# One core, cross attention and max-out FFN: batch 0's tokens by the hardware queue, batch 2's through the array, and one token load per period

## Chip, cores, metric

One core of one Trainium2 chip. The metric is the device time of one execution in microseconds (us). Each kernel was run several times; runs are sorted into a fast and a slow state, and only fast runs are compared. The profile's span is mostly 1.7 to 2.1 us shorter than the time of the same run (168.5 against 170.3 for the kernel before, 158.2 against 160.2 for an experiment), so spans are compared with spans and times with times.

## The reference

```python
# x (8, 8, 512, 64), state (8, 8, 32, 64): batch, head, rows, depth
scores  = softmax(x @ state^T / 8)        ; xread = scores @ state     # 512 rows a batch
scores2 = softmax(state @ x^T / 8)        ; sread = scores2 @ x        # 32 rows a batch
rows = concat(xread, sread), heads side by side  -> (4352, 512)
h = max(rows @ w1, rows @ w2, rows @ w3)  # 512 -> 768
out = h @ w_out                           # 768 -> 512, fp32
```

## The kernel before

The program is a list of small units that are issued in a fixed order; every engine works through its own part of that order. For batch b: `lx` loads the tokens (fp32 in HBM, bf16 in SBUF, a casting DMA issued by POOL); `pm` permutes them in SBUF; then they are transposed, by a DMA on SP's queue (`xb`) or by PE and an eviction (`xT`); `S` makes half the scores, their exponentials `e`, sums and probabilities `a`; `ab` (in a period `X`) transposes the probabilities by a DMA, `aT` by PE; `M b m` folds state and weights into M; `u` is one of three up-projections of a block of 128 hidden columns; `o` half of an output tile; `R` reads the tokens for the state rows.

```python
PERIOD = """
o o u u u u S S o o M M m u R u o u o X u u u u u u u P u u o u o u m M M
"""
...
    def load_x(b):                                    # casting DMA, issued by POOL
        nc.gpsimd.dma_start(
            out=x_sb[:, b].rearrange("p h j d -> p h (j d)"),
            in_=x[b].rearrange("h (p j) d -> p h (j d)", j=J))
...
    def x_crossbar(b):                                # xb: tokens, SP's queue
        nc.sync.dma_start_transpose(
            out=xT(b).rearrange("p j hp t -> p (j hp) t"),
            in_=x_nat(b).rearrange("p j h d -> p (j h d)"))
...
    def a_crossbar(b):                                # ab / X: probabilities, SP's queue
        nc.sync.dma_start_transpose(
            out=aT(b).rearrange("p j a t -> p (j a) t"),
            in_=a_of(b).rearrange("p j a hp n -> p (j a hp n)"))
...
    for t in range(1, B):
        p, g = ORDER[t], ORDER[t + 1]                 # outputs of p, up-projections of g
        nb = t + 2                                    # scores and transposes of nb
        ...
            elif what == "P":
                if nb + 1 < B:
                    permute_x(nb + 1, None, "g")      # a copy on POOL
                    x_crossbar(nb + 1)
            elif what == "X":
                a_crossbar(nb)
```

All eight token loads stand in the opening, before the first period; batch 2's tokens are transposed by a DMA.

The softmax here doesn't subtract the row's maximum and nothing guards it: scores larger than these inputs give would overflow.

Of the kernel before, what the change touches and what calls it, by code (L numbers as in the profile page):

```python
# [8 lines left out]
F32 = mybir.dt.float32  # L9
BF16 = mybir.dt.bfloat16  # L10
# [15 lines left out]


OPENING = """
id, idle 9, sel, idle 9, lx 0, lw 0 1, lx 1, pm 0 0 v, lw 4 6, pm 0 1 g, lw 1 2,
xT 0 0 v, xT 0 1 v, pm 1 0 g, pm 1 1 g, S 0 0 v, M 2 0 aa, S 0 1 v, M 1 0 aa, idle 4,  # L30
lw 2 4, lx 2, M 0 0 aa, aT 0 0 v, R 0, xT 1 0 a, lx 3, aT 0 1 a, xT 1 1 v, S 1 0 g,
u 0 0 0, M 0 4 aa, M 0 5 av, u 0 0 1, u 0 0 2, S 1 1 g, lo, u 0 4 0, u 0 5 0, M 0 1 aa,
u 0 5 1, u 0 4 1, u 0 5 2, M 1 1 aa, u 0 4 2, M 1 4 aa, u 0 1 0, pm 2 - g, aT 1 - v,
xb 2, u 0 1 1, M 0 3 va, M 0 2 va, u 0 1 2, u 1 0 0, u 1 4 0, lx 7, pm 3 - g, u 1 1 0,
lx 6, u 1 0 1, u 0 3 0, u 1 4 1, u 0 2 0, M 1 2 aa, M 1 5 av, xb 3, u 1 4 2, u 0 2 1,
u 1 0 2, u 0 2 2, M 1 3 aa, M 2 3 aa, u 0 3 1, u 0 3 2, u 1 1 1, u 1 2 0, u 1 3 0,
u 1 5 0, u 1 1 2, u 1 5 1, lx 4, u 1 5 2, o 0 0 0 a, o 0 0 1 a, u 1 2 1, S 2 1 g,
S 2 0 g, ab 2, u 1 3 1, o 0 1 0 v, M 2 2 aa, R 1, o 0 1 1 a, o 0 2 0 v, M 2 4 aa,
u 1 2 2, o 0 2 1 a, o 0 3 0 a, M 2 5 aa, M 2 1 va, u 1 3 2, o 0 3 1 v, R 2, lx 5
"""  # L40


PERIOD = """
o o u u u u S S o o M M m u R u o u o X u u u u u u u P u u o u o u m M M
"""
LAST = """
M M u u u M u u S M u u u u u S u u u u P M R M u o u o u u o X o o o o o
"""


# [1 line left out]
def kernel(  # L52
# [14 lines left out]
    nc = tc.nc  # L67

    B, H, S, D = x.shape
# [5 lines left out]
    J = S // 128  # L75
# [6 lines left out]

    const = ctx.enter_context(tc.tile_pool(name="const", bufs=1))
    res = ctx.enter_context(tc.tile_pool(name="res", bufs=1))
    xnp = ctx.enter_context(tc.tile_pool(name="xnp", bufs=3))
    att2 = ctx.enter_context(tc.tile_pool(name="att2", bufs=2))
    tmpp = ctx.enter_context(tc.tile_pool(name="tmpp", bufs=4))
    htp = ctx.enter_context(tc.tile_pool(name="htp", bufs=2))
    op = ctx.enter_context(tc.tile_pool(name="op", bufs=2))
# [3 lines left out]
    def bank(shape, dt, name):  # L93
        return psum.tile(shape, dt, tag="bank", name=name)
# [3 lines left out]
    def copy(eng, o, i):  # L98
        if eng == "a":
            nc.scalar.copy(out=o, in_=i)  # L100
        else:
            ENG[eng].tensor_copy(out=o, in_=i)  # L102

    def mm(out_ap, lhsT, rhs, start, stop, pos=(0, 0)):
        nc.tensor.matmul(out_ap, lhsT, rhs, start=start, stop=stop, tile_position=pos)  # L105

    def tr(out_ap, in_ap):
# [8 lines left out]
    nc.sync.dma_start(  # L116
        out=st32.rearrange("p n d -> p (n d)"),
        in_=state.rearrange("b h (q n) d -> (b h q) (n d)", q=2))
    zeros = const.tile([128, 512], BF16, name="zeros")
    nc.vector.memset(zeros, 0.0)  # L120
    sbd = res.tile([128, B, HP, 2, Ns], BF16, name="sbd")
# [7 lines left out]

    W = res.tile([128, 3, HP, d_ff], BF16, name="W")  # L130
    wout = res.tile([128, MT, d_model], BF16, name="wout")
    x_sb = res.tile([128, B, H, J, D], BF16, name="x_sb")
    M_sb = res.tile([128, B, MT, 2, 3, 128], BF16, name="M_sb")
    AT = res.tile([128, HP, ST], BF16, name="AT")
    w_v = [w.rearrange("(kk p) f -> p kk f", p=128) for w in (moe_w1, moe_w2, moe_w3)]
# [6 lines left out]
    def load_wout():  # L142
        nc.gpsimd.dma_start(out=wout, in_=moe_w_out.rearrange("(kk p) f -> p kk f", p=128))

    def load_x(b):
        nc.gpsimd.dma_start(  # L146
            out=x_sb[:, b].rearrange("p h j d -> p h (j d)"),
            in_=x[b].rearrange("h (p j) d -> p h (j d)", j=J))


# [36 lines left out]
    def tile_of(kind, b, pool, shape):  # L187
        if (kind, b) not in tiles:
            tiles[kind, b] = pool.tile(shape, BF16, tag=kind, name=kind)
        return tiles[kind, b]  # L190

    def x_nat(b):
        return tile_of("xn", b, xnp, [128, J, H, D])

    def xT(b):
        return tile_of("xT", b, att2, [128, J, HP, 128])
# [9 lines left out]

    def permute_x(b, h, eng):
        j = slice(0, J) if h is None else slice(2 * h, 2 * h + 2)
        copy(eng, x_nat(b)[:, j], x_sb[:, b, :, j].rearrange("p h j d -> p j h d"))

    def x_crossbar(b):
        nc.sync.dma_start_transpose(
            out=xT(b).rearrange("p j hp t -> p (j hp) t"),
            in_=x_nat(b).rearrange("p j h d -> p (j h d)"))
# [27 lines left out]
    def a_crossbar(b):  # L242
# [3 lines that stand above are left out]
# [32 lines left out]
    def up(g, m, i):  # L278

        nn = S if g < B else ST  # L280
        ht = tile_of("ht", g, htp, [128, MT, S])
        pw = bank([128, S], F32, "pw")
        if g < B:
            for par in range(2):
                mm(pw, M_sb[:, g, m, par, i, :], aT(g)[:, :, par, :], par == 0, par == 1)
        else:
            for hp in range(HP):
                mm(pw[:, :nn], W[:, i, hp, m * 128:(m + 1) * 128], AT[:, hp, :],
                   hp == 0, hp == HP - 1)
        if i == 0:  # L290
            t = tiles["t", g, m] = tmpp.tile([128, S], BF16, tag="t0", name="t0")
            nc.scalar.copy(out=t[:, :nn], in_=pw[:, :nn])  # L292
        elif i == 1:
            t0 = tiles["t", g, m]
            t = tiles["t", g, m] = tmpp.tile([128, S], BF16, tag="t1", name="t1")
            nc.vector.tensor_max(t[:, :nn], t0[:, :nn], pw[:, :nn])  # L296
        else:
            nc.vector.tensor_max(ht[:, m, :nn], tiles["t", g, m][:, :nn], pw[:, :nn])  # L298

    def out_half(g, j, h, eng):  # L300
        last = g == ORDER[-1]
        if h == 0:
            tiles["po"] = bank([128, d_model], F32, "po")
        po = tiles["po"]
        for kt in range(3 * h, 3 * h + 3):
            mm(po, tiles["ht", g][:, kt, j * 128:(j + 1) * 128], wout[:, kt, :],
               kt == 0, kt == MT - 1)
        if h == 0:
            return
        rows = out[g * SP:g * SP + S, :].rearrange("(p j) f -> j p f", j=J) if g < B else None  # L310
        if last and j == J - 1:
            half = d_model // 2
            for k in range(2):
                o = op.tile([128, half], F32, tag=f"oh{k}", name=f"oh{k}")
                f = slice(k * half, k * half + half)
                copy("av"[k], o, po[:, f])
                (nc.scalar, nc.sync)[k].dma_start(out=rows[j][:, f], in_=o)
            return
        if j % 2 == 0:
            tiles["o"] = op.tile([128, 2, d_model], F32, tag="o", name="o")  # L320
        o = tiles["o"]
        copy(eng, o[:, j % 2, :], po)
        if last:
            nc.sync.dma_start(out=rows[j], in_=o[:, j % 2, :])
        elif g < B:
            if j % 2 == 1:
                nc.sync.dma_start(out=rows[j - 1:j + 1].rearrange("j p f -> p j f"), in_=o)
        else:
            for q in range(4):
                bb = 4 * j + q  # L330
                nc.sync.dma_start(out=out[bb * SP + S:(bb + 1) * SP, :],
                                  in_=o[q * 32:(q + 1) * 32, j % 2, :])
# [46 lines left out]
    for t in range(1, B):  # L379
        p, g = ORDER[t], ORDER[t + 1]  # L380
        nb = t + 2
        us = [(g, m, i) for m in range(MT) for i in range(3)]
        os = [(p, j, h) for j in range(J if p < B else ST // 128) for h in range(2)]
        sc = [0, 1]
        for what in (PERIOD if g != ORDER[-1] else LAST).split():
            if what == "u":
                up(*us.pop(0))
            elif what == "o":
                if os:
                    out_half(*os.pop(0), "a")  # L390
            elif what in ("M", "m"):
                if m_q:
                    m_unit(*m_q.pop(0), "aa" if what == "M" else "av")
            elif nb >= B:
                continue
            elif what == "S":
                scores(nb, sc.pop(0), "g")
            elif what == "P":
                if nb + 1 < B:
                    permute_x(nb + 1, None, "g")  # L400
                    x_crossbar(nb + 1)
            elif what == "R":
                state_reads(nb)
            elif what == "X":
                a_crossbar(nb)
    for j in range(J):
        for h in range(2):
            out_half(ORDER[-1], j, h, "a")
# [29 lines left out]
```

## Time and profile before

| | before |
|---|---|
| time, median (range) | 168.4 us (168.0 to 170.9) |
| span of the profile | 168.5 us (of a run of 170.3 us) |
| PE's longest wait | 7.5 us, for the tokens' DMA transpose `xT` in the opening |
| a steady period | 15.77 us, PE busy 15.66 |
| DMA transposes, median from issue to landing | `xT` 3.8 us, `aT` 3.2 us |

The lines are in the prediction below. A period is bound by PE, the opening by a full DMA and the one transpose that arrives late in it.

### The profile page before, as it was taken

The page shows a single profiled execution, that of the slowest core. Times are in us where ns is not written, and L with a number is a line of the kernel's source. Part 1 is how long each engine was busy: PE and PEld are TensorE (multiplying, and loading weights), DVE is VectorE, ACT ScalarE, POOL GpSimd, SP SyncE. Part 2 cuts the span into 40 slices and gives each one's busy share as a digit, 9 for nine tenths or more (in the row PEclk, how much of TensorE's full clock was granted, in tenths as well). Part 3 has the DMA queues.
Part 4 walks back from the last instruction along what each step waited for, and adds up shares of the span by engine and source line. Part 5 has one row for each costly group of instructions (what it writes and reads, how often), then busy time and mean ns, then how long its engine had stood idle before and what let it go on. Part 6 is the DMA issues. An engine that isn't in the chain of part 4 may idle for free.

```text
span 168.5 us, 3476 instructions
## 1 busy us (share of the span) xinstructions
PE 151.6 (90%) x1353; PEld 74.9 (44%) x1370; DVE 109.0 (65%) x194; ACT 92.9 (55%) x190; POOL 46.7 (28%) x50
## 2 busy tenths in 40 slices
PE   7958999990299989999999999999999999999991
PEld 2435443430243545445445544454455456854440
DVE  2349998971055759949984987498579843559601
ACT  3427987750135286488548755874785473344340
POOL 8876962920060009003500620080013000000000
PEclk9999999998559999999999999999999999999997
DMA  4999999999999904631633382249306033030163
GB/s 133 152 175 196 179 178 197 191 126 126 149 188 146 289 21 160 152 128 69 163 83 124 128 157 67 87 151 168 126 4 187 0 124 127 1 124 0 45 198 132
DMA packets 37536, 21.71 MB, mean 129 GB/s; under 512 B 22672, under 2 KB 34960, under 8 KB 37520
## 3 DMA queue, kind: packets, MB, share of 16 engines
q0 software_dynamic: 15440, 7.34, 35.5%
q1 hardware_dynamic: 21936, 14.03, 33.4%
q8 instruction: 10, 0.16, 0.5%
q10 hardware_dynamic: 144, 0.13, 0.2%
q14 instruction: 6, 0.05, 0.2%
HBM read 15.20 MB, written 8.91 MB: 143 GB/s over the span
## 4 chain that ended last, share of the span: by engine, by line
PE 76%; DMA 16%; POOL 4%; issue 1%; DVE 1%; ACT 1%; POOLq 0%; DVEq 0%; ACTq 0%
PE pw L105 39%; PE po L105 25%; DMA xT<-xn 9%; DMA W<-in_moe_w_dram 7%; PE pm L105 6%; PE pr L105 4%; POOL W L140 2%; PE ps L105 2%; POOL x_sb L146 1%; DVE ht L298 0%; DVE t L296 0%; ACT t L292 0%; PE pa L108 0%; DVE oh L102 0%; ACT oh L100 0%
## 5 line engine op out<-in xcount | busy, mean ns | idle before, releaser
L105 PE MATMUL pw<-aT,M_sb 128*128 128x512 bf16 x288 | 71.3, 381 | 0.1
L105 PE MATMUL po<-wout,ht 128*128 128x512 bf16 x189 | 50.9, 384 | 1.0 <-issue 0.3
L296 DVE TENSOR_TENSOR t<-t,pw 128x512 bf16<-128x512 bf16 (+1 forms) x54 | 35.1, 652 | 22.4 <-ACT t L292 14.0
L292 ACT CAST t<-pw 128x512 bf16<-128x512 f32 (+1 forms) x54 | 30.1, 570 | 27.8 <-PE pw L105 27.5
L105 PEld LDWEIGHTS <-M_sb 128*128 128x128 bf16 x288 | 26.5, 98 | 32.5 <-issue 3.7
L298 DVE TENSOR_TENSOR ht<-t,pw 128x512 bf16<-128x512 bf16 (+1 forms) x54 | 35.3, 657 | 7.1 <-PE pw L105 3.4
L100 ACT CAST M_sb<-pm 128x384 bf16<-128x384 f32 x81 | 33.2, 504 | 5.3 <-PE pm L105 5.3
L238 POOL TENSOR_TENSOR a<-e,rden 128x512 bf16<-128x512 bf16 x14 | 14.4, 1044 | 73.0 <-ACT e L230 46.8
L100 ACT COPY o<-po 128x512 f32<-128x512 f32 x32 | 19.1, 596 | 21.1 <-PE po L105 16.4
L105 PEld LDWEIGHTS <-ht 128*128 128x128 bf16 x204 | 19.3, 99 | 22.7 <-issue 2.9
L102 POOL COPY xn<-x_sb 128x2048 bf16<-128x2048 bf16 (+1 forms) x9 | 15.1, 1687 | 7.4 <-DMA x_sb<-in_x_dram 7.2
L230 ACT ACTIVATE e<-ps 128x512 bf16<-128x512 f32 x16 | 9.0, 605 | 13.0 <-PE ps L105 12.9
L234 DVE TENSOR_REDUCE den<-e 128x16 f32<-128x512 bf16 x16 | 10.6, 663 | 8.5 <-ACT e L230 8.3
L105 PE MATMUL pm<-W,sbd 64*32 64x384 bf16 x384 | 12.7, 331 | 0.6 <-DVE ht L298 0.4
L105 PE MATMUL ps<-sbd,xT 128*128 128x64 bf16 x128 | 5.8, 199 | 7.6 <-DMA xT<-xn 7.5
L105 PEld LDWEIGHTS <-xT 128*128 128x128 bf16 x128 | 5.2, 102 | 9.8 <-DMA xT<-xn 8.0
L105 PEld LDWEIGHTS <-sbd 64*32 64x32 bf16 x384 | 4.3, 90 | 10.9 <-issue 10.2
L140 POOL DMA_DIRECT2D W<-in_moe_w_dram x12 | 9.0, 766 | 0.0
L105 PE MATMUL pw<-AT,W 128*128 128x256 bf16 x72 | 8.8, 273 | 0.0
L102 DVE CAST M_sb<-pm 128x384 bf16<-128x384 f32 x15 | 7.8, 529 | 1.3 <-PE pm L105 1.3
L271 DVE RECIPROCAL rd<-pr 128x128 f32<-128x128 f32 x8 | 7.6, 950 | 1.6 <-PE pr L105 1.4
L105 PE MATMUL pz<-zeros 128*128 128x512 bf16 x20 | 6.9, 495 | 1.2 <-DVE zeros L120 1.2
(38 smaller groups left out, 66.3 us busy)
## 6 DMA issues: line engine op xcount, KB each, us to landing
out_dram<-o SPq DMA_DIRECT2D x14, 512.0 KB, 2.6
x_sb<-in_x_dram POOLq DMA_DIRECT2D x8, 512.0 KB, 10.4
W<-in_moe_w_dram POOLq DMA_DIRECT2D x6, 256.0 KB, 8.2
W<-in_moe_w_dram POOLq DMA_DIRECT2D x6, 128.0 KB, 8.0
wout<-in_moe_w_out_dram POOLq DMA_DIRECT2D x1, 768.0 KB, 12.0
out_dram<-o SPq DMA_DIRECT2D x3, 256.0 KB, 2.1
st<-in_state_dram SPq DMA_DIRECT2D x1, 512.0 KB, 3.4
out_dram<-o SPq DMA_DIRECT2D x8, 64.0 KB, 1.7
```

The lines of the kernel that those rows point to most:

```text
L100: nc.scalar.copy(out=o, in_=i)
L102: ENG[eng].tensor_copy(out=o, in_=i)
L105: nc.tensor.matmul(out_ap, lhsT, rhs, start=start, stop=stop, tile_position=pos)
L140: nc.gpsimd.dma_start(out=W[:, i, :, c], in_=w_v[i][:, :, c])
L146: nc.gpsimd.dma_start(out=x_sb[:, b].rearrange("p h j d -> p h (j d)"), in_=x[b].rearrange("h (p j) d -> p h (j d)", j=J))
L230: nc.scalar.activation(out=e.rearrange("p r n -> p (r n)"), in_=ps.rearrange("p j a hp n -> p (j a hp n)"), func=AF.Exp, scale=scale)
L234: nc.vector.reduce_sum(out=den, in_=e, axis=AX.X)
L238: ENG[eng].tensor_mul(out=a_of(b)[:, 2 * h:2 * h + 2].rearrange("p j a hp n -> p (j a hp) n"), in0=e, in1=rden.unsqueeze(2).to_broadcast(( ...
L271: nc.vector.reciprocal(out=rd, in_=pd.rearrange("p (hp n) -> p hp n", hp=HP))
L292: nc.scalar.copy(out=t[:, :nn], in_=pw[:, :nn])
L296: nc.vector.tensor_max(t[:, :nn], t0[:, :nn], pw[:, :nn])
L298: nc.vector.tensor_max(ht[:, m, :nn], tiles["t", g, m][:, :nn], pw[:, :nn])
```

## The change

Its intent: take the late transpose away (batch 2 through the array), start earlier (batch 0 by the free hardware queue), and free the DMA in the opening (batches 4 to 7 are loaded one per period). Cut to its core (the opening's order, not shown in full, moves many units, and the last period's order changes too; four token buffers in place of eight):

```diff
 OPENING
-id, idle 9, sel, idle 9, lx 0, lw 0 1, lx 1, ... xb 2, ... lx 7, ... lx 6, ... lx 4, ... lx 5
+id, idle 9, sel, idle 9, pm 0 1 v, pm 0 0 a, ... lx 1, ... lx 2, ... lx 3, ... xT 2 1 v, ... xT 2 0 a, ...
 PERIOD
-o o u u u u S S o o M M m u R u o u o X u u u u u u u P u u o u o u m M M
+L u S u o S P u u o u o u u u u u o u o o u u m M m u X R o u u o u m m m u
+    xlp = ctx.enter_context(tc.tile_pool(name="xlp", bufs=4))
+    x32 = res.tile([128, H, J, D], F32, name="x32")
+    nc.sync.dma_start(out=x32.rearrange("p h j d -> p h (j d)"),
+                      in_=x[0].rearrange("h (p j) d -> p h (j d)", j=J))
     def load_x(b):
+        x_sb[b] = xlp.tile([128, H, J, D], BF16, tag="x", name="x")
         nc.gpsimd.dma_start(
-            out=x_sb[:, b].rearrange("p h j d -> p h (j d)"),
+            out=x_sb[b].rearrange("p h j d -> p h (j d)"),
     def permute_x(b, h, eng):
-        copy(eng, x_nat(b)[:, j], x_sb[:, b, :, j].rearrange("p h j d -> p j h d"))
+        i = x_sb[b][:, :, j] if b else x32[:, :, j]
+        copy(eng, x_nat(b)[:, j], i.rearrange("p h j d -> p j h d"))
+            elif what == "L":
+                if nb + 1 < B:
+                    load_x(nb + 1)
```

Note two things in the new period: `L` comes first in the text, and `P` (permute and transpose of the next batch's tokens) now comes ahead of `X` (transpose of the probabilities).

More of the change, by code (lines that the diff above doesn't have):

```diff
@@ L28 @@
 OPENING = """
-id, idle 9, sel, idle 9, lx 0, lw 0 1, lx 1, pm 0 0 v, lw 4 6, pm 0 1 g, lw 1 2,
-xT 0 0 v, xT 0 1 v, pm 1 0 g, pm 1 1 g, S 0 0 v, M 2 0 aa, S 0 1 v, M 1 0 aa, idle 4,
-lw 2 4, lx 2, M 0 0 aa, aT 0 0 v, R 0, xT 1 0 a, lx 3, aT 0 1 a, xT 1 1 v, S 1 0 g,
-u 0 0 0, M 0 4 aa, M 0 5 av, u 0 0 1, u 0 0 2, S 1 1 g, lo, u 0 4 0, u 0 5 0, M 0 1 aa,
-u 0 5 1, u 0 4 1, u 0 5 2, M 1 1 aa, u 0 4 2, M 1 4 aa, u 0 1 0, pm 2 - g, aT 1 - v,
-xb 2, u 0 1 1, M 0 3 va, M 0 2 va, u 0 1 2, u 1 0 0, u 1 4 0, lx 7, pm 3 - g, u 1 1 0,
-lx 6, u 1 0 1, u 0 3 0, u 1 4 1, u 0 2 0, M 1 2 aa, M 1 5 av, xb 3, u 1 4 2, u 0 2 1,
-u 1 0 2, u 0 2 2, M 1 3 aa, M 2 3 aa, u 0 3 1, u 0 3 2, u 1 1 1, u 1 2 0, u 1 3 0,
-u 1 5 0, u 1 1 2, u 1 5 1, lx 4, u 1 5 2, o 0 0 0 a, o 0 0 1 a, u 1 2 1, S 2 1 g,
-S 2 0 g, ab 2, u 1 3 1, o 0 1 0 v, M 2 2 aa, R 1, o 0 1 1 a, o 0 2 0 v, M 2 4 aa,
-u 1 2 2, o 0 2 1 a, o 0 3 0 a, M 2 5 aa, M 2 1 va, u 1 3 2, o 0 3 1 v, R 2, lx 5
+id, idle 9, sel, idle 9, pm 0 1 v, pm 0 0 a, xT 0 0 v, xT 0 1 v, lx 1, idle 3, pm 1 1 v,
+lw 4 6, lw 0 1, pm 1 0 v, lw 2 4, S 0 0 g, lx 2, S 0 1 g, xT 1 1 a, R 0, xT 1 0 a,
+S 1 1 g, S 1 0 g, lw 1 2, lo, M 1 5 aa, M 0 5 aa, aT 0 0 v, aT 0 1 v, M 0 4 aa, M 1 0 av,
+M 0 0 vv, u 0 5 0, aT 1 - v, u 0 4 0, M 2 4 av, M 1 4 aa, u 0 5 1, lx 3, u 0 0 0,
+u 0 4 1, u 0 5 2, u 1 0 0, M 0 2 va, M 0 3 aa, u 0 0 1, u 0 0 2, pm 2 - g, u 1 0 1,
+u 0 2 0, M 1 3 aa, u 0 4 2, u 0 2 1, u 1 4 0, u 0 3 0, u 0 3 1, M 0 1 aa, u 1 4 1,
+xT 2 1 v, u 1 3 0, M 2 5 va, M 1 2 aa, pm 3 - g, u 1 0 2, u 1 4 2, u 0 1 0, xT 2 0 a,
+u 1 5 0, u 0 3 2, u 0 2 2, u 0 1 1, u 1 2 0, u 0 1 2, S 2 0 g, xb 3, M 2 0 aa, M 1 1 aa,
+u 1 3 1, u 1 2 1, o 0 0 0 v, S 2 1 g, o 0 0 1 v, u 1 5 1, M 2 2 aa, u 1 1 0, u 1 5 2,
+o 0 1 0 v, ab 2, o 0 1 1 a, R 1, u 1 3 2, u 1 1 1, o 0 2 0 a, u 1 1 2, u 1 2 2,
+o 0 2 1 a, M 2 1 av, M 2 3 aa, R 2, o 0 3 0 a, o 0 3 1 a
 """
 PERIOD = """
-o o u u u u S S o o M M m u R u o u o X u u u u u u u P u u o u o u m M M
+L u S u o S P u u o u o u u u u u o u o o u u m M m u X R o u u o u m m m u
 """
 LAST = """
-M M u u u M u u S M u u u u u S u u u u P M R M u o u o u u o X o o o o o
+X u u u u u u u M u u L u P u u u o o u M M M R u S u u S M o u o o M o o o
 """
@@ L131 @@
     wout = res.tile([128, MT, d_model], BF16, name="wout")
-    x_sb = res.tile([128, B, H, J, D], BF16, name="x_sb")
     M_sb = res.tile([128, B, MT, 2, 3, 128], BF16, name="M_sb")
@@ L143, in load_wout @@
         nc.gpsimd.dma_start(out=wout, in_=moe_w_out.rearrange("(kk p) f -> p kk f", p=128))
+    x_sb = {}
     def load_x(b):
+        x_sb[b] = xlp.tile([128, H, J, D], BF16, tag="x", name="x")
         nc.gpsimd.dma_start(
-            out=x_sb[:, b].rearrange("p h j d -> p h (j d)"),
+            out=x_sb[b].rearrange("p h j d -> p h (j d)"),
             in_=x[b].rearrange("h (p j) d -> p h (j d)", j=J))
@@ L313, in out_half @@
             for k in range(2):
-                o = op.tile([128, half], F32, tag=f"oh{k}", name=f"oh{k}")
+                o = res.tile([128, half], F32, name=f"oh{k}")
                 f = slice(k * half, k * half + half)
```

## The prediction

> **What bounds the kernel now.** I read the page's slices first, then the chain of work that ended last, then who waited for whom, then the stages in windows, then the DMA views.
>
> ```profile
> PE   7958999990299989999999999999999999999991
> PEclk9999999998559999999999999999999999999997
> DMA  4999999999999904631633382249306033030163
> ```
>
> Each slice is 4.2 us. PE is full except at the start and in slices 10 and 11 (38 to 46 us), after which its clock falls to half. The DMA engines are full from 4 to about 58 us, and mostly free afterwards. So there is one hole, at the end of a stage in which the DMA is saturated. The chain and the waits of PE say what the hole is:
>
> ```profile
> 29.69 0.55 PE pw L105 x3
> 30.24 14.89 DMA xT<-xn
> 45.17 1.03 PE ps L105 x16
> ...
> PE ps L105 <- DMA xT<-xn: 7.5, 1, 7.5
> ```
>
> The scores of batch 2 wait 7.5 us for their transposed tokens, which a DMA transpose, issued at 30.2 us, delivers only 15 us later. The queue table and the issues say why (columns: size, median us from issue to landing):
>
> ```profile
> q0 software_dynamic: 15440, 7.34, 35.5%
> q1 hardware_dynamic: 21936, 14.03, 33.4%
> ...
> x_sb<-in_x_dram POOLq DMA_DIRECT2D x8, 512.0 KB, 10.4
> ...
> xT<-xn SPq DMA_TRANSPOSE x6, 3.8
> ```
>
> A transpose usually lands in 3.8 us; this one shared the engines with the casting loads of batches 7 and 6, queued at 30 to 35 us, which nobody needs for another 40 us or more. The stages (columns: length, then busy time of PE, PEld, DVE, ACT, POOL, then clock, DMA and GB/s):
>
> ```profile
> 9.94:37.68 27.74, 26.48 (x290) 12.56 (x292) 24.10 (x42) 20.02 (x43) 18.67 (x19) 1.00 1.45 178
> 37.68:45.17 7.49, 0.01 (x2) 0.01 (x1) 0.69 (x1) 0.20 (x1) 0.00 (x0) 0.69 1.50 132
> 45.17:56.46 11.29, 10.96 (x120) 5.62 (x121) 6.35 (x12) 5.22 (x11) 2.93 (x3) 0.75 1.29 177
> 56.46:72.94 16.48, 15.94 (x151) 7.54 (x149) 12.65 (x23) 8.66 (x18) 3.87 (x3) 1.00 0.47 137
> 72.94:88.71 15.77, 15.66 (x155) 7.43 (x149) 12.05 (x22) 10.58 (x23) 3.88 (x3) 1.00 0.41 117
> ```
>
> These are the opening before the hole, the hole, the rest of the opening, the first period and a steady one. A period is PE-bound: 15.66 of 15.77 us.
>
> **PE's work at full clock**, from the start-to-start times of full runs in the chain: a up-projection pair of matmuls ("u") 0.431 us (18 matmuls in 3.88), an output half ("o") 0.647, a unit of M 0.203 (24 pm in 0.61), a half of scores 0.235, the state reads of a batch 0.81, an array transpose of half a batch 0.45, of the probabilities 0.41 a batch, a filler matmul 0.216. A period is 18 u, 8 o, 6 M, 2 S and 1 R: 7.76 + 5.18 + 1.22 + 0.47 + 0.81 = 15.4 us, against 15.77 measured; 0.3 us are gaps. The opening from its first array transpose (9.94 us) on holds 36 u, 8 o, 18 M, 6 S, 3 R, 4 array halves, two batches of probabilities and 4 fillers: 31.7 us. It took 46.5 us (9.94 to 56.46). Of the 14.8 us lost, 7.5 are the hole; the half clock after it made 8.1 us of work last 11.3, so 3.2; some 4.1 are lost before the hole, where DVE is 87% busy and the weights are still arriving.
>
> **What the Trainium skill says.** "TensorE: Matmul & The Clock Gate", Part 1, says that the array drops to half clock after an idle window of about 3.4 us and needs about as long a busy one to recover. The trace agrees: after 7.5 us without a matmul the granted clock is 0.55 in 40 to 45 us and 0.50 in 45 to 50 us. "DMA: Bandwidth & Descriptors", Issuing engines are not separate DMA queues, says that DMAs of all engines run on the same 16 DMA engines and interleave; the trace agrees (15 us against 3.8 us for the same transpose). The same page, SWDGE vs HWDGE vs iDMA, says that only a GpSimd DMA can cast, so tokens that come by the hardware queue must be cast on the core; all casting loads of the trace are on POOL's queue. "VectorE: DVE Perf Modes", The perf-mode tier table, gives 1227 ns for an fp32 copy of 2048 elements in SBUF; for the half batch of 1024 I estimate from it 0.7 us. The trace has no such copy, but ACT's fp32 cast of 128x1024 took 1.04 us.
>
> **The change, part by part.**
>
> *Batch 2 through the array.* It removes the DMA transpose that PE waited for. It adds two array halves, 0.9 us of PE and 0.69 us of DVE plus 1.0 us of ACT for the evictions. Removed: 7.5 us of hole and, as no idle of over 3.4 us should remain, the 3.2 us of half clock. Net about -9.8 us.
>
> *Loads of batches 4 to 7 one per period.* The software queue moved four token loads (1024 packets each), all the weights and w_out by 50 us. From the landings I read (batch 0 at 9.5 us, the third weight group at 18.4, batch 2 at 28.3) it serves 1000 packets in about 2.4 us after a start near 6.6 us. The new opening asks 9984 packets of it, so it is done at some 30 to 32 us. Batch 2 lands at 22 to 25 us; PE reaches its transposes at about 26 to 28. Batch 3 lands at 30 to 32, its permute takes 1.9 us on POOL, and its transpose, now in free engines, 3.8: it lands by 38, and PE asks for it at about 45. In the periods a load has no producer to wait for, so POOL issues it right after the previous permute, some 8 to 10 us before its own permute; with free engines I expect it to land in 6 to 8 us. Nothing on the path, but close.
>
> *Batch 0 by the hardware queue.* The state's 0.5 MB was issued at 0.74 us and landed 3.4 us later; 1 MB behind it should land at 7 to 8 us (twice the bytes at about the state's rate, beside the first software load). The casts take 0.7 us (DVE) and 1.05 us (ACT), side by side. So the first array transpose starts near 8.6 us instead of 9.94: 1.3 us sooner. But what follows needs weights: the first M units need 2560 packets (13 to 15 us), the third kind 4096 (16 to 18.5). DVE has some 10 us of work of its own before the first u, too. I put the first u at about 17.5 us, where it was 17.6, but with 5.4 us of PE work done before it, 0.2 us more than before.
>
> *The order.* After the first u the new opening has 32.35 - 5.6 = 26.8 us of PE work and about 24 us of DVE (36 us listed in all by unit durations, 10 before the first u, times 0.945 because instructions overlap in the trace). With some 1 to 1.5 us of gaps it ends at 45 to 46 us. Before, it ended at 56.5. That is -10.5 to -11.5: the 9.8 of the first part, and about 1 from a better order. In the periods three more M copies go from ACT to DVE: 3 x 0.53 brings DVE to 13.6 of 15.8 us, ACT down to 9.1. PE remains the bound; I leave the period at 15.8 us. Before, five periods took 79.5 us (the first one 0.7 longer), and from 136.0 to the end 32.5. Sum: 45.7 + 79.5 + 32.5 = 157.7; with 0.2 from the profile to the median (168.5 to 168.7) and a little for the risks below, 158.3 us.
>
> **Rivals.** *The hole only moves.* The weights wanted late (units of M 1) land at 26 to 28 us, and PE reaches them at about the same time; or 1 MB of fp32 delays all of the software queue by up to 2.4 us (1024 packets' time), and PE stands at the first M units. For it: the DMA engines stay full until 30 us. Against it: PE's order puts each weight group as late as it can. It would cost 2 to 4 us, and a gap over 3.4 us the half clock again: 161 to 164 us. *DVE becomes the bound.* In the new period it is at 86%, and reductions stand between maxima in its one queue; the opening has it over 90%. If every period slipped by 0.5 us, 2.5 to 3 us: 161 us. *Loads in the periods collide* with the two transposes and the stores, as in the old opening: a late token load delays the permute, this the transposes behind it on SP's queue, and the probabilities of the next batch come late at the head of the next period. For it: its first u is now PE's first work of the period, and the transpose of the probabilities stands behind that of the tokens. Against it: the DMA row has free engines in the periods, a load needs about 2.4 us of all of them, and I count over 3 us of slack. At 1 us in each of five periods, 163 us. *No gain at all* would need the hole to be hidden slack: but PE is the bound before and after it, so I give this little.
>
> **Range and chances.** The removed 10.7 us (hole and half clock) are sure unless another wait takes their place; the rivals cost 2 to 5 us each and seldom come together. Better than planned: the opening could lose 2 us less than I give it. So 155.5 to 162.5 us in 8 of 10; over 2% faster means under 165.3 us, which needs less than a third of the 10.7: 0.95. Within 2%: 0.04; slower: 0.01.
>
> **What would show it.** Right: no PE wait for the token transpose over 1 us, no slice of clock under 0.9 before the end, the opening's end (first period's scores) near 46 us, periods of 15.5 to 16, DMA engines free from about 32 us, first array transpose at 8 to 9 us. Wrong: PE waits for W or for xT before 30 us that sum to over 3 us; periods over 16.2 with DVE or a DMA as releaser; a token load over 10 us in the periods.

## The result, and the profile after

The changed kernel is slower: 176.3 and 176.6 us in its two fast runs (two more runs, 180.0 and 180.3, were of the slow state), against a median of 168.4. The ratio is 1.046, 95% interval 1.035 to 1.056. (Ratios are the mean time of one kernel's fast runs over that of the other's of the same rounds, so not quite the ratio of the medians quoted.)

The slices of the changed kernel, 4.4 us each:

```profile
PE   7895999999899945999459997799999999999990
...
PEclk9999999999999997899956999999999999999998
DMA  5999999257931994039940299309611530230253
```

The hole of the opening is gone, and so is most of the DMA's saturation: it is full until 31 us only. But three new holes stand near 65, 87 and 108 us, each under a stretch of full DMA, and the clock falls after the first two. Who PE waited for:

```profile
PE pw L106 <- DMA aT<-a: 11.2, 4, 4.6
```

The transposed probabilities, 11.2 us in four waits, the longest 4.6. The stages (length, busy time of PE, PEld, DVE, ACT, POOL, then clock, DMA, GB/s), each period cut in two at the moment when the transpose of the probabilities is issued (in the second and third period PE has done somewhat less by then, 59 and 56 matmul records against 67):

```profile
47.22:57.42 10.20, 10.14 (x67) 4.83 (x76) 6.73 (x12) 5.32 (x10) 4.79 (x4) 1.00 0.27 88
57.42:67.09 9.67, 5.69 (x88) 2.56 (x75) 6.76 (x13) 4.53 (x10) 0.00 (x0) 1.00 1.35 196
67.09:78.72 11.63, 11.41 (x59) 5.40 (x60) 6.55 (x12) 5.20 (x9) 4.79 (x4) 0.85 0.20 47
78.72:89.27 10.55, 5.92 (x89) 2.69 (x89) 6.97 (x13) 4.53 (x10) 0.00 (x0) 0.93 1.39 174
89.27:101.09 11.82, 11.60 (x56) 5.44 (x58) 6.40 (x11) 4.61 (x8) 4.79 (x4) 0.77 0.18 45
101.09:110.03 8.94, 6.66 (x92) 2.88 (x90) 7.21 (x13) 5.12 (x11) 0.00 (x0) 1.00 1.36 213
110.03:125.80 15.77, 15.66 (x146) 7.48 (x149) 11.61 (x21) 9.11 (x18) 3.91 (x3) 1.00 0.45 94
```

The opening ends at 47.2 us, 9.3 earlier than before. Then three periods take 19.9, 22.2 and 20.8 us in place of 15.8: 15.5 us lost. The fourth takes 15.77 again, and it is the first one in which no load is issued. What happens on the queues in the first of them (POOL, then SP; start, time in issue, what):

```profile
52.83 1.89 POOL L103 COPY xn<-x 128x2048 bf16<-128x2048 bf16 x1
54.66 0.94 POOL L153 DMA_DIRECT2D x<-in_x_dram  x1
```

```profile
54.74 1.32 SPq L220 DMA_TRANSPOSE xT<-xn  x1
56.11 1.21 SPq L335 DMA_DIRECT2D out_dram<-o  x1
57.42 4.69 SPq L251 DMA_TRANSPOSE aT<-a  x1
```

POOL issues the load of the next batch (`L` of the next period) as soon as its permute is done, since that load waits for nothing else. SP issues the transpose of the tokens at the same moment, since it waits for the same permute. A store and the transpose of the probabilities follow within 2.7 us. The chain shows what PE gets of it:

```profile
57.42 9.62 DMA aT<-a
67.09 0.85 PE pw L106 x2
```

9.6 us from issue to landing, where this transpose took 3.2 in the median before; PE's first up-projection of the next period needs it. The tokens' transpose and the load itself are as slow (54 to 68 us; size, us from issue to landing):

```profile
x<-in_x_dram POOLq DMA_DIRECT2D x1, 512.0 KB, 11.3
xT<-xn SPq DMA_TRANSPOSE x1, 9.5
```

In the second period the probabilities took 10.5 us, in the third 8.9.

### The profile page after: what moved, and what is told of

The parts are those of the page before. It is cut to its first block, busy times and chain, and to the rows that moved or that the text cites. A ratio compares the mean times of both kernels' runs of the same rounds, so it can differ in the third digit from the quotient of the medians.

```text
span 174.5 us, 3505 instructions
## 1 busy us (share of the span) xinstructions
PE 153.5 (88%) x1368; PEld 76.0 (44%) x1385; DVE 116.8 (67%) x212; ACT 90.7 (52%) x175; POOL 44.6 (26%) x48
## 4 chain that ended last, share of the span: by engine, by line
PE 64%; DMA 27%; POOL 3%; issue 2%; ACT 1%; DVE 1%; POOLq 0%; DVEq 0%
PE pw L106 36%; DMA aT<-a 21%; PE po L106 21%; DMA W<-in_moe_w_dram 5%; PE pm L106 3%; PE ps L106 2%; POOL a L246 2%; POOL x L153 1%; PE pr L106 1%; PE px L109 1%; ACT M_sb L101 0%; PE pa L109 0%; DVE den L242 0%; ACT e L238 0%; DVE oh L103 0%
## 5 line engine op out<-in xcount | busy, mean ns | idle before, releaser
L106 PE MATMUL pw<-aT,M_sb 128*128 128x512 bf16 x288 | 76.3, 389 | 11.2 <-DMA aT<-a 11.2
L106 PE MATMUL po<-wout,ht 128*128 128x512 bf16 x188 | 52.3, 385 | 1.2 <-issue 0.4
L246 POOL TENSOR_TENSOR a<-e,rden 128x512 bf16<-128x512 bf16 x16 | 16.6, 1042 | 73.0 <-issue 30.8
L101 ACT CAST M_sb<-pm 128x384 bf16<-128x384 f32 x64 | 26.6, 495 | 2.2 <-PE pm L106 2.1
L103 DVE CAST M_sb<-pm 128x384 bf16<-128x384 f32 x32 | 16.2, 551 | 1.2 <-PE pm L106 0.8
L103 POOL COPY xn<-x 128x2048 bf16<-128x2048 bf16 x6 | 11.4, 1892 | 9.2 <-PE pw L106 6.8
L106 PE MATMUL pm<-W,sbd 64*32 64x384 bf16 x384 | 11.9, 327 | 1.1 <-ACT M_sb L101 1.0
L106 PEld LDWEIGHTS <-xT 128*128 128x128 bf16 x128 | 6.7, 108 | 5.3 <-issue 1.9
L106 PEld LDWEIGHTS <-W 128*128 128x128 bf16 x72 | 7.0, 98 | 2.5
L106 PE MATMUL ps<-sbd,xT 128*128 128x64 bf16 x128 | 7.3, 206 | 0.9 <-ACT xT L101 0.9
```

Of the source, the lines that this page charges most:

```text
L101: nc.scalar.copy(out=o, in_=i)
L103: ENG[eng].tensor_copy(out=o, in_=i)
L106: nc.tensor.matmul(out_ap, lhsT, rhs, start=start, stop=stop, tile_position=pos)
L246: ENG[eng].tensor_mul(out=a_of(b)[:, 2 * h:2 * h + 2].rearrange("p j a hp n -> p (j a hp) n"), in0=e, in1=rden.unsqueeze(2).to_broadcast(( ...
```

## The experiments

Two theories at the start. Theory 1: the load, issued at the same moment as the transposes, makes them late. Theory 2: the new order alone is too late, because the transpose of the probabilities stands behind that of the tokens and a store on SP's queue. Ten kernels were run, one of them twice (v1_again), all at several rounds. The ratio in a row is to the kernel before on the same chip; the median is that of all runs.

| run | fast runs over those of before (95% interval) | median us | PE's waits for `aT`, us | `aT` issue to landing, median us |
|---|---|---|---|---|
| changed kernel | 1.046 (1.035 to 1.056) | 178.3, fast 176.3 and 176.6 | 11.2 | 8.4 |
| e1_no_load (wrong result) | 0.946 (0.940 to 0.953) | 160.2 | 0 | 4.1 |
| m1_half_load (wrong result) | 0.965 (0.958 to 0.972) | 164.1 | 3.5 | 6.1 |
| e2_loads_first | 0.958 (0.949 to 0.966) | 162.0 | 0 | 4.9 |
| e3_x_first | 0.961 (0.953 to 0.969) | 162.8 | 0.5 | 3.1 |
| v1_sp_behind | 0.943 (0.936 to 0.949) | 160.4 | 0 | 4.1 |
| v2_late_load | 0.956 (0.949 to 0.964) | 162.7 | 1.6 | 4.8 |
| v3_act_beside | 1.011 (1.008 to 1.014) | 171.9, fast 169.5 to 172.0 | 6.1 (a slow run) | 4.7 (a slow run) |
| v4_x0_soft | 0.959 (0.953 to 0.965) | 162.8 | 0 | 4.2 |
| b1_array2 | 0.974 (0.966 to 0.983) | 165.2 | 1.4 | 3.3 |
| b2_load_per_period | 0.967 (0.958 to 0.978) | 164.6 | 1.8 | 3.2 |

### e1_no_load: the loads of the periods left out

```diff
             elif what == "L":
                 if nb + 1 < B:
-                    load_x(nb + 1)
+                    x_sb[nb + 1] = x_sb[3]
```

> The changed kernel with the four token loads of the periods left out; batches 4 to 7 read batch 3's tokens, so the result is wrong on purpose, and every instruction of PE, DVE, ACT and every DMA transpose stays. Theory 1 (the load, issued by POOL at the moment SP issues the two transposes, makes the transpose of the probabilities late): the transposes land in about 3 to 4 us, PE's waits for aT fall from 11.2 us to under 1, every period is about 15.8 us, and the time is 158 to 160 us, my prediction's sum. Theory 2 (the new order alone is too late: the transpose of the probabilities stands behind that of the tokens and behind a store in SP's queue): PE still waits several us for aT in each period, time over 168 us.

Measured: 160.2 us, span 158.2, no wait of PE for any transpose in the periods. SP's queue in the first period:

```profile
53.92 1.33 SPq L220 DMA_TRANSPOSE xT<-xn  x1
55.30 0.68 SPq L335 DMA_DIRECT2D out_dram<-o  x1
56.08 1.90 SPq L251 DMA_TRANSPOSE aT<-a  x1
```

The same three transfers in the same order as in the changed kernel, but the third is issued in 1.9 us, not 4.7, and lands in 4.4 us, not 9.6 (in all periods 3.1 to 5.7):

```profile
aT<-a SPq DMA_TRANSPOSE x1, 4.4
```

Theory 2 falls: order, engines and instructions are the changed kernel's own. The four loads cost it all of 16.3 us of span (174.5 - 158.2), and without them it runs as predicted, but for a constant (see the first point on the prediction below).

What the DMA engines do in the collision is worth a look. First the changed kernel from 54 to 68 us, 0.35 us a slice, then e1 from 53 to 62 us, 0.23 us a slice:

```profile
DMA  0000015999999799999999999999999332999980
GB/s 0 0 0 0 0 44 138 213 224 218 169 139 87 66 109 75 121 137 157 158 166 159 177 211 301 345 385 297 247 191 111 105 91 64 277 448 374 433 340 12
```

```profile
DMA  0000000003999999999997988999980000000000
GB/s 0 0 0 0 0 0 0 0 0 90 288 291 290 289 290 291 291 443 404 400 382 273 455 214 151 216 204 229 198 193 16 0 0 0 0 0 0 0 0 0
```

Without the load, the tokens' transpose runs at 290 GB/s, the store at 400, the probabilities at 200. With it, the engines are just as full, but move mostly 70 to 220 GB/s for 6 us: the load does not only add its bytes, what runs beside it moves more slowly too. (The load is counted here with the 0.5 MB that it writes. It reads 1 MB of fp32, so a part of the gap is its reading.) In the first of the two windows, the load's packets took 36.0% of 14 us, 5.0 us of all 16 engines. I had reckoned with 2.4; but that was the pace of the queue in the opening, and the packet times of different queues overlap (here the shares add up to 105.8%), so the two are not the same measure.

### m1_half_load: the dose

```diff
             elif what == "L":
                 if nb + 1 < B:
-                    load_x(nb + 1)
+                    x_sb[nb + 1] = x_sb[3]
+                    half = xlp.tile([128, H // 2, J, D], BF16, tag="half", name="half")
+                    nc.gpsimd.dma_start(out=half..., in_=x[nb + 1, 0:H // 2]...)
```

(One token buffer fewer, three.)

> The changed kernel with its loads in the periods at half their size (512 packets), into a tile that nobody reads, the tokens of batch 3 being used instead: a wrong result on purpose. Theory 1, with the delay in proportion to the load: the transpose of the probabilities takes 6 to 7 us in place of 8 to 10, about 1 us too late or in time; PE's waits for aT fall from 11.2 to 0 to 3 us, time 160 to 163 us. If any concurrent load makes the transposes slow at a fixed price: still over 170 us.

Measured: 164.1 us. The median landing of `aT` goes 4.1, 6.1, 8.4 us for no, half and a full load: some 2.1 us for each 256 KB. PE's waits go 0, 3.5, 11.2: not in proportion, because a landing of up to some 6 us is waited for by nobody. In the three periods concerned the landings are 4.4 to 5.7 us with no load, 7.2 to 7.6 with half a load and 8.9 to 10.5 with a full one. The wait was a little longer than I had allowed (3.5 against 0 to 3) and the time 1 us over the range. There is no fixed price.

### e2_loads_first: the loads back in the opening

```diff
-... u 0 5 1, lx 3, u 0 0 0,
+... u 0 5 1, lx 3, lx 4, lx 5, lx 6, lx 7, u 0 0 0,
-    xlp = ... bufs=4
+    xlp = ... bufs=6
             elif what == "L":
-                if nb + 1 < B:
-                    load_x(nb + 1)
+                pass
```

> The changed kernel with loads 4 to 7 queued in the opening, right behind load 3, as the kernel before had them (six token buffers in place of four, as seven don't fit). Theory 1: periods of 15.8 us and no PE wait for aT after the first period; the opening gets a share of the old trouble, because the transposes of batch 3's tokens and batch 2's probabilities now run beside the loads until about 42 us: 160 to 166 us. Theory 2: still over 168 us.

Measured: 162.0 us with a right result, no wait for `aT` at all. The opening's transposes were late (12.3 us for batch 3's tokens) but not waited for, because batch 2 goes through the array. So the loads in the opening, which the change took away as harmful, are nearly harmless once batch 2's transpose is out of their way; undoing this one part turns 4.6% slower into 4% faster.

### e3_x_first: the probabilities ahead of the tokens

```diff
-L u S u o S P u u o u o u u u u u o u o o u u m M m u X R o u u o u m m m u
+L u S u o S X P u u o u o u u u u u o u o o u u m M m u R o u u o u m m m u
```

> The changed kernel with the transpose of the probabilities moved ahead of the tokens' permute and transpose in the period (X before P), loads unchanged. Both theories: it is issued some 2 us before the load and lands before it takes the engines, so the wait for aT at the head of the period goes. Theory 1 adds that the transpose of the tokens still runs beside the load and takes 9 to 10 us, which is 16 to 17 us after the period's start where 16.2 are to be had: a wait of up to 1 us for xT in three periods, 159 to 163 us. Theory 2: no such wait, 158 to 159 us.

Measured: 162.8 us, right result. SP now issues the probabilities when the second half is ready and the tokens 1.8 us later, when the load is issued as well. From the queues of SP and of POOL:

```profile
53.41 1.25 SPq L251 DMA_TRANSPOSE aT<-a  x1
55.24 2.36 SPq L220 DMA_TRANSPOSE xT<-xn  x1
```

```profile
55.16 0.94 POOL L153 DMA_DIRECT2D x<-in_x_dram  x1
```

`aT` lands in 3.1 us, `xT` in 9.2, and PE waits 1.3 us for `xT` in two periods. Both transposes suffer from the load when they run beside it; what it costs depends on which of them PE wants first. This is the order of the kernel before, and it is why one load per period looked safe there.

### v1_sp_behind: fp32 loads behind the transposes, on the same queue

```diff
+    def load_f(b):
+        x_sb[b] = xfp.tile([128, H, J, D], F32, tag="xf", name="xf")
+        nc.sync.dma_start(out=x_sb[b]..., in_=x[b]...)
-L u S u o S P u u o u o u u u u u o u o o u u m M m u X R o u u o u m m m u
+u S u o S P u u o u o u u u u u o u o o u u m M m u X L R o u u o u m m m u
             elif what == "L":
-                if nb + 1 < B:
-                    load_x(nb + 1)
+                if nb + 2 < B:
+                    load_f(nb + 2)
```

(`lf 4` stands behind `ab 2` in the opening; three bf16 token buffers in place of four, one fp32 buffer more.)

> The changed kernel with the tokens of batches 4 to 7 loaded like those of batch 0: 1 MB of fp32 by SP's hardware queue, issued right behind the transpose of the probabilities, one batch earlier than before, and cast by POOL in its permute. Theory 1: a load behind the transposes in the same queue can't delay them, so aT lands in 4 to 6 us as without loads, PE's waits for aT are under 1 us, periods about 15.8 us, and the time is 160 to 161.5 us with a right result; POOL's permute from fp32 may take longer than 1.9 us without harm. If what hurts is any load in the period, 165 us or more.

Measured: 160.4 us, right result, no wait for a DMA transpose, 5.7% faster than the kernel before: the best of all runs with a right result. SP's queue:

```profile
57.06 1.72 SPq L258 DMA_TRANSPOSE aT<-a  x1
58.87 0.84 SPq L154 DMA_DIRECT2D xf<-in_x_dram  x1
```

Twice the bytes written into SBUF, one after the other with the transposes, cost next to nothing: 0.2 us over e1, which loads nothing in the periods (on another chip; relative to the kernel before 0.943 against 0.946). This run changes the queue, the type and the moment of the load at once; the next one changes its moment. POOL's permute from fp32 takes 1.89 us, as from bf16.

### v2_late_load: the same casting load, later

```diff
             elif what == "L":
-                if nb + 1 < B:
-                    load_x(nb + 1)
+                if nb + 2 < B:
+                    nc.gpsimd.tensor_copy(out=late, in_=tiles["ht", g][:, 4, 0:1])
+                    load_x(nb + 2)
-L u S ... m M m u X R o u u o u m m m u
+u S ... m M m u X R o u L u o u m m m u
```

> The changed kernel with the same casting loads on POOL's queue, of the same size and number, one batch earlier and held back by a copy of one element on POOL that reads a late column of ht, so that they are issued some 14 us into the period, after the transpose of the probabilities has landed, and not with the two transposes. Theory 1 (the moment of the load is what hurts, not the load): PE's waits for aT under 1 us (0.5 at the first period, whose load stays where it was), periods about 15.8 us, 160 to 162 us. If a load anywhere in the period costs as much: 170 us or more.

Measured: 162.7 us, 0.7 over the range. The casting load on POOL's queue does little harm when it comes later, so it is the moment that counts. One period still lost 1.6 us: the load issued at 62.0 us landed in 8.3 us and the permute waited 2.0 us for it, which made both transposes of that period late (PE's only wait for a transpose, 1.6 us). I had put the delayed load too close to its user.

### v3_act_beside: an fp32 load beside the transposes, on ACT's hardware queue

```diff
-        nc.sync.dma_start(
+        nc.scalar.dma_start(
-u S u o S P u u o u o u u u u u o u o o u u m M m u X L R o u u o u m m m u
+u S u o S P u u o u o u u u u u L o u o o u u m M m u X R o u u o u m m m u
```

(The diff is to v1. The two fp32 buffers are also shared here by batch 0 and the loads, where v1 has one for each.)

> v1_sp_behind with its fp32 loads issued by ACT's hardware queue about when SP issues the two transposes, so beside them and not behind them. If any load of that size beside the transposes, of whatever queue, makes them late (the 16 engines are shared): the transpose of the probabilities takes 7 to 9 us and PE waits for it by several us in all, 163 to 170 us. If it takes the casting software queue: 4 to 5 us, no wait, 160 to 161.5 us.

Measured: 171.9 us; its fast runs (169.5 to 172.0) are 1.1% slower than the kernel before, and some 7% slower than v1, of which it differs in the queue and the moment of four loads and in the sharing of their buffers. The time, slightly above the range, speaks against the casting and POOL's queue as the only cause: a load on a hardware queue of its own at that moment costs about two thirds as much (some 7% over v1, where the changed kernel with its casting loads is some 11% over it). The run that was profiled counts as slow, but by little: it took 172.05 us, the slowest fast run 171.95. Its trace agrees:

```profile
PE pw L107 <- DMA aT<-a: 6.1, 3, 2.1
```

In its periods the tokens' transpose lands in 7.3 to 9.1 us beside a load and in 4.2 without one; that of the probabilities takes 4.8 to 9.8 us and is issued late, SP having been held 3.9 us in a store and 5.5 us in a transpose. But the clock also falls once in the opening of this run, for about a slice, and no fast run was traced, so how the 11 us divide is not shown.

### b1_array2: the kernel before with batch 2 through the array

```diff
-xb 2, u 0 1 1, ... M 1 5 av, xb 3, u 1 4 2, u 0 2 1, u 1 0 2, u 0 2 2,
+u 0 1 1, ... M 1 5 av, u 1 4 2, u 0 2 1, u 1 0 2, xT 2 1 v, xb 3, u 0 2 2,
-u 1 1 1, u 1 2 0,
+u 1 1 1, xT 2 0 a, u 1 2 0,
```

> The kernel before with only batch 2's tokens sent through the array (two array halves in place of its DMA transpose), loads unchanged. If the hole of 7.5 us and the half clock after it were due to that transpose alone: about 10 us less, less 1 us for the added work and its evictions: 159 to 161 us. If the hole only moves (the transposes of batch 3's tokens and batch 2's probabilities also run beside the queued loads until 50 us): 164 to 168 us, with PE waiting for xT or aT at the head of the first period.

Measured: 165.2 us, the verdict unclear at 2% (0.974, 0.966 to 0.983). The wait for `xT` is gone, but the hole partly moves. PE waits 1.4 us for `aT`, and then for ACT, which waits for an output buffer whose store was stuck in the full queues:

```profile
54.27 0.59 ACT L100 COPY o<-po 128x512 f32<-128x512 f32 x1 [7.00 <-DMA out_dram<-o]
```

ACT stood 7.0 us for a store issued at 45.5 us. Of the 10 us that the hole and the half clock cost, this part alone gives back some 4.

### b2_load_per_period: the kernel before with one load per period

```diff
-... lx 7, ... lx 6, ... lx 4, ... lx 5
+... (only lx 0 to lx 3 in the opening)
-o o u u u u S S o o M M m u R ...
+L o o u u u u S S o o M M m u R ...
+            elif what == "L":
+                if nb + 1 < B:
+                    load_x(nb + 1)
```

> The kernel before with one part alone: token loads 4 to 7 leave the opening and come one per period, issued by POOL right after the permute; its old order (the transpose of the probabilities ahead of that of the tokens) stays. The hole of the opening shrinks, because batch 2's transpose then runs beside load 3 and the output weights only: I expect 2 to 4 us of it left. In the periods the transpose of the tokens takes 9 to 10 us, from 7.5 us into the period, and is asked for 18.8 us into it: no wait. So 160 to 163 us. If loads in the periods hurt whatever the order: 168 us or more.

Measured: 164.6 us, 1.6 above the range. PE's wait for batch 2's transpose shrinks from 7.5 to 1.2 us; a wait of 1.8 us for `aT` at the head of the first period is new. In the periods:

```profile
62.16 9.11 DMA xT<-xn
71.31 0.64 PE ps L105 x16
```

The tokens' transpose takes 9.1 us beside the load, as in the other kernels, but PE asks for it so late that it waits 0.35 us, once; the next three periods take 15.8 us (scores at 71.31, 87.09, 102.86 and 118.63 us). So one load per period is a gain in the old order, and a loss only together with the new one. I had put the need for `xT` 11 us after its issue; in this first period it was under 9.

### v1_again and v4_x0_soft: batch 0's queue alone

```diff
-    x32 = res.tile([128, H, J, D], F32, name="x32")
-    nc.sync.dma_start(out=x32..., in_=x[0]...)
-id, idle 9, sel, idle 9, pm 0 1 v,
+id, idle 9, sel, idle 9, lx 0, pm 0 1 v,
```

(The diff is to v1; the buffers are fitted to it.)

> The version of v1_sp_behind once more, as the reference of this chip for the two runs beside it: 160 to 161 us again.

> v1_sp_behind with batch 0's tokens by the casting software queue ahead of batch 1's, as in the kernel before: that part of the change alone is undone. My prediction gave it a first array transpose 1.3 us sooner, but no sooner first up-projection. By that, the first transpose comes near 10 us, batch 1 and the weights some 2.4 us later than in v1, PE stands 1 to 2 us longer in the opening, and the time is 161 to 163 us. If batch 0's queue does not matter: within 0.5 us of v1.

Measured side by side: 160.4 us for v1, 162.8 with batch 0 by the software queue (ratios to the kernel before 0.947 and 0.959, intervals 0.941 to 0.953 and 0.953 to 0.965). The first array transpose came at 10.34 us, in v1_again at 8.71. So the hardware queue for batch 0 is worth about 2 us. (Executions of equal mean clock say the same: at 1.00, 161.7 and 162.3 us against 159.6 to 160.5.)

## Why the prediction was wrong, point by point

- **What bounds the kernel before: right.** Hole, half clock and periods are as read; removing the hole was worth what was said. e1, the changed kernel less its loads, has a span of 158.2 us; my sum for the span was 157.7. The step from the span to the time was wrong: I added 0.2 us, the median of 168.7 less the span of 168.5, but that span belongs to a run of 170.3 us. Between the span and the time of one run lie some 2 us, so e1 took 160.2 us where I had 158.3.
- **Batch 2 through the array: right in mechanism.** No wait for it is left. b1 shows that it gives only some 4 us by itself: the other 6 need the loads out of the opening's end too, or an order that doesn't mind them (e2).
- **Batch 0 by the hardware queue: right, and worth more than said.** First array transpose at 8.54 us (predicted 8.6), DVE's fp32 copy 0.694 us (the estimate of 0.7 from the skill's tier table holds), ACT's 1.046. First up-projection at 18.2 us (17.5 predicted). I gave this part nothing in the end; v4 gives it 2 us.
- **The order: right within 1 to 2 us.** I put the opening's end at 45 to 46 us; it came at 47.2, and at 46.5 without the loads. (The work before the first up-projection is 5.4 us in one sum and 5.6 in the next; this is within that.) DVE did not become the bound: PE was busy 15.66 of 15.77 us in the period without a load.
- **Loads in the periods: the step that failed.** It read: "with free engines I expect it to land in 6 to 8 us. Nothing on the path, but close." Three things were wrong in it. First, the engines are not free then: the load is released by the same permute as the tokens' transpose, 0.08 us apart (54.66 and 54.74). I had written that POOL issues the load right after the permute, which is also what the tokens' transpose waits for, and did not set the two times side by side. Second, the load took 9.5 to 12.0 us in the periods, not 6 to 8, and each transpose beside it 8.9 to 10.5 us, not 3 to 4. Third, the transpose of the probabilities was issued 10.2 us into the period and was due at 15.8. That leaves 5.6 us for it to land: 2.4 us of slack with the 3.2 us of the kernel before, not the "over 3 us of slack" that I counted. In e1, without any load, the slowest took 5.7 us of some 6. And the load had no need to be sent then: it was not 8 to 10 us ahead of its own permute but 19 (54.66 and 73.73 us), and 13.6 in the rhythm of e1 (from the end of one permute, 53.90, to the next, 67.53).
- **The rival was named, and mis-sized.** "Loads in the periods collide" gave 1 us in each of five periods. The runs show 4.1, 6.4 and 5.0 us in three periods (19.87, 22.18, 20.76 less 15.77). Its path was not the one I gave, either: no permute in the periods waited for a load; the transposes themselves ran slowly beside it. Two of my own signs of being wrong came true, periods over 16.2 us with a DMA as releaser and loads over 10 us. Of the 16.3 us between the changed kernel and e1, 11.2 are PE's waits, about 4.5 the half clock after two of them (1.7 us of work lost in 11.63 us at a mean clock of 0.85, 2.7 in 11.82 at 0.77), and some 0.6 are left.
- **The half clock again.** I had said that no idle time of over 3.4 us should remain. Two waits of 3.9 and 4.6 us did, and the clock fell after each of the first two; after the third, of about 2.2 us, it stayed at 1.00. The clock was at half for an estimated 3.5 and 5.4 us of the work after them, and for 5.6 after the hole of the kernel before (from the mean clocks 0.85, 0.77 and 0.75 over 11.63, 11.82 and 11.29 us), so the "about as long" of the prediction is short for two of three. The fall is what "TensorE: Matmul & The Clock Gate", Part 1, says of an idle window of some 3.4 us. A long wait is not the only way to it: in e2_loads_first and v1_again the clock is at 0.50 from 18 to 20 us, though PE waited nowhere in these runs for more than 1.2 us; it had been busy for 2.1 and 2.4 of the 4 us before (14 to 18 us). The changed kernel, with nearly the same opening, stayed at 1.00 there in its trace. Part of the spread between executions is this: in v1_again the two at a mean clock of 0.989 took 161.5 and 162.0 us, the four at 1.00 159.6 to 160.5.

What stays open: why mixed traffic is so much slower than the sum of its parts (70 to 220 GB/s against 290 and 400), and how v3's loss divides. The slow state of two of the changed kernel's four runs was not studied.

## What to carry to other kernels

A load that waits for no producer was issued here the moment its queue came to it (54.66 us); ask what else the same event releases, and write the two times side by side. A prefetch that nobody needed for 19 us did harm because it ran beside a transfer that PE needed within 6. Put behind that transfer in the same queue, as in v1_sp_behind, it cost next to nothing. Judge a part of a change in the order in which it will stand: one load per period was a gain in the old order and cost 16 us in the new one.

## What the Trainium skill lacked or had wrong

- "DMA: Bandwidth & Descriptors", Issuing engines are not separate DMA queues: it says that DMAs share the 16 engines and interleave; it has no number for a DMA transpose beside a plain load. Here a 256 KB transpose takes 4.4 to 5.7 us, 7.2 to 7.6 and 8.9 to 10.5 beside no, a 256 KB and a 512 KB casting load (e1, m1, the changed kernel), with the engines full and moving mostly 70 to 220 GB/s where the transpose of the tokens alone moves 290.
- The same page, Rules for kernel authors: "A transpose next to ordinary DMAs needs nothing" holds for the data (every run that loaded all tokens was correct), but it says nothing of the time: 9.6 us here, 4.4 for the same transpose in e1.
- The same page's rule to issue a DMA early and wait late lacks the other side: four loads issued early cost 16.3 us of span here, and next to nothing when issued behind the transposes (v1 160.4 us, e1 without these loads 160.2).
- No number was found for how long a transpose holds the issuing queue while the DMA is busy: SP spent 4.69 us in the issue of one transpose beside a load, and 1.90 us in the same place without.
